# Cosine attention and a leaky-ReLU layer: a re-ordered opening, and the q and k of four batches turned on TensorE

## The chip, the cores and the metric

The kernel runs on one core of one Trainium2 chip. The metric is device time in microseconds (us). The kernel before took 509.25 us (median of 3 runs, 507.22 to 510.2).

Engines are named as in the profile: PE is TensorE (PEld its weight loads), DVE is VectorE, ACT is ScalarE, POOL is GpSimd, SP issues DMAs. In these traces each engine works through its own instructions in the order of the program (run 9 shows it for ScalarE); that is the key to most of what follows.

## The reference

```python
# q, k, v: (8 batches, 12 heads, 448 rows, 64); tau = 0.1
q_n = q / (norm(q) + 1e-6);  k_n = k / (norm(k) + 1e-6)
scores = q_n @ k_n.T / tau                      # per batch and head, 448 x 448
attn = softmax(scores);  x = attn @ v           # then heads side by side: (3584, 768)
h = x @ w_in                                    # (768, 2048)
out = maximum(0.01 * h, h) @ w_out              # (2048, 768) -> (3584, 768)
```

## The kernel before

Each batch goes through: load q, k, v (cast to bf16 by the DMA); normalise q and k (sums of squares on DVE, roots on ACT, products on POOL or DVE); turn q and k so that the 64 elements of a head lie on partitions; scores on PE; exponentials on ACT; column sums and products with V on PE; x on DVE. The two dense layers run on PE between the half-steps of the attention of a later batch. A batch has 12 half-steps, n = 0 to 11, each half of a pair of heads; four heads are a quad (three quads, g = 0 to 2).

```python
def load_w_in(a):                       # 8 transfers in all
    for s in range(2):
        nc.gpsimd.dma_start(out=w_in_sb[32*a : 32*a+32, s::2, :], in_=w_in_r[a, :, :, s, :])

def turn(b, what):                      # by DMA, a whole batch of q or k
    nc.sync.dma_start_transpose(out=xt[...], in_=xn.rearrange("p g t h d -> p (g t h d)"))

def turn_pair(b, p):                    # on PE, one pair of heads of q and k: 8 matmuls, 2 DVE copies
    tp = pmm.tile([128, 2, NT, PK], BF16, name="mm")
    ...                                 # nc.tensor.matmul(..., rhs=ident, is_transpose=True)
    nc.vector.tensor_copy(out=xt[:, g, :, j, :], in_=tp[:, i])

def weigh(b, g, s):
    if s == 0:
        sm = ppv.tile(...);  columns(sm, b, g, ones)      # 16 matmuls: the sums
        st["rs"] = wk.tile(...);  nc.vector.reciprocal(st["rs"], sm)
    po = ppv.tile(...)                                    # ppv has 2 buffers
    columns(po, b, g, v of the quad)                      # 16 matmuls: the values
    nc.vector.tensor_mul(x[:, 2*g+s, ...], po, rs)

# [... the opening: batch 0 in quads, turned by turn_pair ...]
weigh(0, 0, 0);  scores(0, 2, 1);  weigh(0, 0, 1);  scores(0, 3, 0)
# [...]
weigh(0, 2, 0);  weigh(0, 2, 1);  fill(2.0)       # three groups of the first dense layer

def second(n):                          # what batch 1 does besides: it prepares batch 2
    # [...]
    elif n == 8:
        norm_inverse(2, "q");  norm_apply(2, "q", POOL);  norm_root(2, "k")
    elif n == 9:
        norm_inverse(2, "k");  norm_apply(2, "k", DVE, step=4);  turn(2, "q")
    elif n == 10:
        turn(2, "k")

def later(b, n):                        # the same for batches 2 to 7
    if n == 0:   norm_sums(b + 1, "q")
    elif n == 1: norm_root(b + 1, "q")
    elif n == 2: load(b + 1, "v");  norm_sums(b + 1, "k");  norm_inverse(b + 1, "q");  norm_apply(b + 1, "q", POOL)
    # [... n == 3, 4: root, inverse and product of k; n == 5: turn q; n == 7: turn k ...]

# [... in every half-step n of batch b: scores; then one weigh of an earlier quad, if owed;
#      then second(n) or later(b, n); then dense groups ("fill") ...]
```

## Time and profile before

I mark progress by the start of the first exponential of each batch (in the list of ACT's instructions every 24th exponential):

| kernel before | us |
|---|---|
| batch 0 | 15.9 |
| batch 1 | 61.8 |
| batch 2 | 127.2 |
| batch 3 | 185.6 |
| batch 7 | 404.3 |
| end | 506.9 |

From batch 2 to batch 6 a batch takes 51.5 to 58.4 us. Batch 1 takes 65.4, although it has the shorter dense work. The page of the profiled execution shows where. The first line is each engine's busy time; the other two are busy tenths of TensorE, and the tenths of its clock granted, in 40 slices of 12.7 us.

```profile
PE 433.9 (86%) x3296; PEld 205.9 (41%) x3296; DVE 210.8 (42%) x218; ACT 266.0 (52%) x429; POOL 127.8 (25%) x152
...
PE   0566789850899998999799998999799999998996
...
PEclk9998699985899999999899999999999999999999
```

TensorE is near full from the twelfth slice on. It is poorly used in the first five, and the tenth shows 0: a hole from 107.9 to 126.6 us. What ended its idle times (engine and line, who released it: us in total, times, longest) names it:

```profile
PE sc L198 <- DMA kT<-k_n: 18.8, 1, 18.8
...
PE pv L209 <- DVE rs L231: 8.1, 5, 2.3
...
PE mm L253 <- DVE xT L242: 6.7, 3, 2.5
...
PE mm L172 <- POOL k_n L144: 4.3, 1, 4.3
...
PE mm L253 <- DVE xT L239: 0.9, 2, 0.4
```

The chain of waits around the hole (start, us, what):

```profile
103.21 4.97 POOL q_n L144 x3
...
108.28 3.21 SPq L161
...
113.12 13.46 DMA kT<-k_n
...
126.62 0.93 PE sc L198 x3
```

GpSimd finishes q of batch 2 at 108.2. Then SP issues the DMA that turns q, two small output stores, and at 113.12 the DMA that turns k; that one lands 13.46 us later, and only then can the scores of batch 2 begin. k itself had been normalised on DVE by 106.3; its turn waited in SP's queue.

The opening, in the timeline (start, duration, engine, line, operation, tiles, count; in brackets the idle time before it and who ended it):

```profile
25.17 0.82 POOL L90 DMA_DIRECT2D qk_bf<-in_k_dram  x1 [0.91 <-DMA w_in_sb<-in_moe_w_in_dram]
...
26.09 2.05 POOL L144 TENSOR_TENSOR k_n<-qk_bf,k_ni 112x512 bf16<-112x512 bf16 x2
...
27.21 0.55 PE L172 MATMUL mm<-ident,k_n 112*128 112x112 bf16 x4 [4.27 <-POOL k_n L144]
...
31.35 2.96 DVE L231 RECIPROCAL rs<-pv 128x448 f32<-128x448 f32 x1 [0.84 <-PE pv L209]
...
34.36 0.94 PE L209 MATMUL pv<-pe,v_bf 112*32 112x448 bf16 x16 [1.39 <-DVE rs L231]
...
35.67 3.34 ACT L202 ACTIVATE pe<-sc 112x896 bf16<-112x896 f32 x4 [1.12 <-PE sc L198]
```

GpSimd issues loads until 25.98, each behind the landing of an earlier weight transfer. Only then comes its next arithmetic, the normalisation of k of the second quad, and TensorE waits 4.27 us for it. At 31.35 the reciprocal of the first quad starts; the second values of the quad need the bank that it reads (one of the two buffers of `ppv` that TensorE writes to), so TensorE's queue stands until 34.36 and the next scores, and ScalarE behind them, with it.

### The profile page before, as it was taken

What the parts mean: (1) busy time and instruction counts of PE and PEld (TensorE: products, weight loads), DVE (VectorE), ACT (ScalarE), POOL (GpSimd) and SP (SyncE); (2) the same over time, 40 slices, a digit from 0 to 9 for tenths busy, and PEclk for the clock granted to TensorE, in tenths of its full rate; (3) what the DMA queues carried; (4) which work ended last, traced back from release to release, by engine and by line L of the source; (5) the groups of instructions that cost most, each with busy time, mean ns of one, the idle gap of its engine ahead of it and who ended that gap; (6) DMA issues with size and microseconds to landing.
All of it is one profiled execution on the core that took longest, in us unless ns stands there. A gap on an engine that the chain in (4) does not pass through costs nothing.

```text
span 506.9 us, 7801 instructions
## 1 busy us (share of the span) xinstructions
PE 433.9 (86%) x3296; PEld 205.9 (41%) x3296; DVE 210.8 (42%) x218; ACT 266.0 (52%) x429; POOL 127.8 (25%) x152
## 2 busy tenths in 40 slices
PE   0566789850899998999799998999799999998996
PEld 0232345420243453445234544444334544453463
DVE  4657577930760328332930367235633033203000
ACT  3746275530377446755566346744665557552411
POOL 7375343160046001810173004500350000000000
PEclk9998699985899999999899999999999999999999
DMA  9999948139226925293429524611442210020022
GB/s 120 212 199 203 201 57 110 31 62 199 41 43 106 135 63 87 56 163 79 71 54 120 108 51 68 104 53 49 54 78 54 60 45 1 17 60 19 1 62 64
DMA packets 79395, 42.59 MB, mean 84 GB/s; under 512 B 35072, under 2 KB 78592, under 8 KB 79360
## 3 DMA queue, kind: packets, MB, share of 16 engines
q0 software_dynamic: 37760, 22.81, 32.9%
q1 hardware_dynamic: 41600, 19.28, 17.2%
q8 instruction: 26, 0.43, 0.3%
q14 instruction: 9, 0.07, 0.0%
HBM read 45.61 MB, written 11.01 MB: 112 GB/s over the span
## 4 chain that ended last, share of the span: by engine, by line
PE 65%; DVE 13%; DMA 7%; ACT 6%; issue 4%; POOL 2%; SPq 1%; DVEq 0%; ACTq 0%; POOLq 0%
PE mm L253 25%; PE mm L265 24%; PE pv L209 10%; PE sc L198 6%; DVE rs L231 5%; ACT pe L202 3%; DMA w_in_sb<-in_moe_w_in_dram 3%; DMA kT<-k_n 3%; DVE q_ni L121 2%; DVE k_ni L121 2%; DVE q_n L112 2%; ACT hT L257 2%; POOL q_n L144 2%; DMA qk_bf<-in_q_dram 1%; DVE k_n L112 1%
## 5 line engine op out<-in xcount | busy, mean ns | idle before, releaser
L202 ACT ACTIVATE pe<-sc 112x896 bf16<-112x896 f32 x192 | 165.2, 918 | 34.0 <-PE sc L198 34.0
L253 PE MATMUL mm<-xT,w_in_sb 128*128 128x384 bf16 (+1 forms) x768 | 160.0, 359 | 13.7 <-DVE xT L242 6.7
L231 DVE RECIPROCAL rs<-pv 128x448 f32<-128x448 f32 x24 | 71.0, 2958 | 203.1 <-PE pv L209 203.1
L265 PE MATMUL mm<-w_out_sb,hT 128*128 128x384 bf16 x896 | 153.5, 327 | 0.1
L265 PEld LDWEIGHTS <-hT 128*128 128x128 bf16 x896 | 84.7, 98 | 68.5 <-issue 15.2
L253 PEld LDWEIGHTS <-w_in_sb 128*128 128x128 bf16 x768 | 72.5, 99 | 95.6 <-issue 36.6
L257 ACT ACTIVATE hT<-mm 128x384 bf16<-128x384 f32 (+1 forms) x128 | 68.9, 546 | 68.1 <-PE mm L253 67.6
L271 ACT COPY osb<-mm 128x384 f32<-128x384 f32 x56 | 26.8, 479 | 108.0 <-PE mm L265 81.2
L198 PE MATMUL sc<-qT,kT 64*128 64x448 bf16 (+1 forms) x384 | 58.6, 374 | 27.5 <-DMA kT<-k_n 18.8
L144 POOL TENSOR_TENSOR q_n<-qk_bf,q_ni 112x512 bf16<-112x512 bf16 x44 | 47.5, 1108 | 81.6 <-DVE q_ni L138 49.7
L209 PE MATMUL pv<-pe,v_bf 112*32 112x448 bf16 x768 | 48.0, 370 | 8.1 <-DVE rs L231 8.1
L90 POOL DMA_DIRECT2D v_bf<-in_v_dram x8 | 7.6, 946 | 141.8 <-PE pv L209 141.8
L144 POOL TENSOR_TENSOR k_n<-qk_bf,k_ni 112x512 bf16<-112x512 bf16 x40 | 40.5, 1043 | 11.1 <-DVE k_ni L138 8.5
L198 PEld LDWEIGHTS <-kT 64*128 64x128 bf16 (+1 forms) x384 | 14.6, 105 | 64.7 <-issue 42.7
L209 PEld LDWEIGHTS <-v_bf 112*32 112x32 bf16 x768 | 19.6, 100 | 30.4 <-issue 19.8
L121 DVE TENSOR_REDUCE q_ni<-q_n 112x16 f32<-112x1024 bf16 (+1 forms) x12 | 27.4, 2284 | 0.3
L121 DVE TENSOR_REDUCE k_ni<-k_n 112x16 f32<-112x1024 bf16 (+1 forms) x12 | 27.4, 2284 | 0.3
L209 PE MATMUL pv<-pe,ones 112*32 112x448 bf16 x384 | 25.5, 382 | 0.6 <-ACT pe L202 0.6
L242 DVE TENSOR_TENSOR xT<-pv,rs 128x448 bf16<-128x448 f32 x24 | 14.9, 621 | 8.7 <-PE pv L209 7.4
L239 DVE TENSOR_TENSOR xT<-pv,rs 128x384 bf16<-128x384 f32 x24 | 13.4, 557 | 12.3 <-PE pv L209 11.0
L172 PE MATMUL mm<-ident,q_n 112*128 112x112 bf16 x48 | 5.1, 240 | 12.8 <-DVE q_n L144 12.3
L209 PEld LDWEIGHTS <-ones 112*32 112x32 bf16 x384 | 8.4, 99 | 15.7 <-issue 12.2
(44 smaller groups left out, 129.6 us busy)
## 6 DMA issues: line engine op xcount, KB each, us to landing
v_bf<-in_v_dram POOLq DMA_DIRECT2D x8, 672.0 KB, 7.5
qk_bf<-in_q_dram POOLq DMA_DIRECT2D x6, 672.0 KB, 10.2
qk_bf<-in_k_dram POOLq DMA_DIRECT2D x6, 672.0 KB, 13.4
w_in_sb<-in_moe_w_in_dram POOLq DMA_DIRECT2D x8, 384.0 KB, 14.8
w_out_sb<-in_moe_w_out_dram POOLq DMA_DIRECT2D x2, 1536.0 KB, 22.8
out_dram<-osb SPq DMA_DIRECT2D x16, 168.0 KB, 2.2
out_dram<-osb SPq DMA_DIRECT2D x16, 144.0 KB, 2.0
out_dram<-osb SPq DMA_DIRECT2D x16, 120.0 KB, 1.9
```

The costliest lines, as they stand in the source:

```text
L112: eng.tensor_mul(sq, x, x)
L121: nc.vector.tensor_reduce(st[what + "i", b][:, 4 * g0 : 4 * g1], squares(b, what, g0, g1), axis=AX.X, op=ALU.add,)
L144: eng.tensor_tensor(out=xn[:, g, :, a : a + step, :].rearrange("p t h d -> p h t d"), in0=x[:, h : h + step], in1=ni[:, h : h + step].unsq ...
L198: nc.tensor.matmul(out=sc[:wide, a, :S], lhsT=kT[r, o : o + wide], rhs=q5[r, g, :, j, :], start=True, stop=True,)
L202: nc.scalar.activation(out=pe[:, ki], in_=sc[:PK, :, :S], func=ACTF.Exp, scale=inv_tau)
L209: nc.tensor.matmul(out=dst[32 * a : 32 * a + 32, :], lhsT=weights(a, ki), rhs=st["pe", b, 2 * g + a // 2][:, ki, a % 2, :], start=(ki == 0 ...
L231: nc.vector.reciprocal(st["rs"], sm)
L242: nc.vector.tensor_mul(x[:, kt, 64:512], po, rs)
L253: nc.tensor.matmul(out=pm[:, :n], lhsT=w_in_sb[:, kt, m * 128 : (m + 1) * 128], rhs=st["x", c][:, kt, :n], start=(kt == 0), stop=(kt == KT ...
L257: nc.scalar.activation(out=st["h", c][:, m, :n], in_=pm[:, :n], func=ACTF.Prelu, alpha=0.01)
L265: nc.tensor.matmul(out=po[:, :NH], lhsT=st["h", c][:, m, j0 : j0 + 128], rhs=w_out_sb[:, m, n * NH : (n + 1) * NH], start=(m == 0), stop=( ...
L271: nc.scalar.copy(out=osb, in_=po[:, :NH])
```

## The change

The intent: shorten the opening and remove the hole.

```diff
-    w_in_r = moe_w_in.rearrange("(g a s j) n -> a j g s n", g=G, a=4, s=2)
+    w_in_r = moe_w_in.rearrange("(a c j) n -> a j c n", a=4, c=KT)   # a quad is now heads g, 3+g, 6+g, 9+g
     def load_w_in(a):
-        for s in range(2):
-            nc.gpsimd.dma_start(
-                out=w_in_sb[32 * a : 32 * a + 32, s::2, :], in_=w_in_r[a, :, :, s, :]
-            )
+        nc.gpsimd.dma_start(out=w_in_sb[32 * a : 32 * a + 32], in_=w_in_r[a])
# [... norms, sums and products follow the new quads ...]
     norm_root(0, "q", 0, 1)
-    norm_squares(0, "q", A, 1, 2)
     norm_root(0, "k", 0, 1)
# [...]
-    weigh(0, 0, 0)
+    sm = sums(0, 0)
+    po = values(0, 0, 0)
+    inverse(0, 0, sm)
     scores(0, 2, 1)
-    weigh(0, 0, 1)
+    load_w_out(0)
+    x_write(0, 0, 0, po)
     scores(0, 3, 0)
+    x_write(0, 0, 1, values(0, 0, 1))
# [... the second quad likewise ...]
-    weigh(0, 2, 0)
-    weigh(0, 2, 1)
-    fill(2.0)
+    for m in (0, 1):
+        layer1(0, m, 0, 4)             # two dense groups, the contraction's first 4 parts of 6
+    sm = sums(0, 2)
+    po = psc.tile([128, 2, 512], F32, name="sc")
+    for s in (0, 1):
+        values(0, 2, s, po[:, s, :S])
+    inverse(0, 2, sm)
+    for s in (0, 1):
+        x_write(0, 2, s, po[:, s, :S])
+    for m in (0, 1):
+        layer1(0, m, 4, KT)            # and the last 2
# [... batch 1, n == 8 ...]
+                norm_root(2, "k")
+                norm_inverse(2, "q")
+                norm_inverse(2, "k")
+                for g in range(G):
+                    norm_apply(2, "q", P, g, g + 1)
+                    norm_apply(2, "k", V if g == 0 else P, g, g + 1)
-            turn(2, "q")
-            turn(2, "k")
# [... batch 3: sums of q at n == 3, of k at n == 5, products at n == 6 of batch 2 ...]
+    turns = {                          # (batch, half-step): (batch to turn, pairs...)
+        (1, 3): (1, 2), (1, 4): (1, 3), (1, 5): (1, 4, 5), (1, 10): (2, 0, 1),
+        (1, 11): (2, 2, 3), (2, 1): (2, 4, 5), (2, 9): (3, 0, 1), (2, 10): (3, 2, 3),
+        (2, 11): (3, 4, 5),
+    }
-        wide = 128 if b > 1 else PK
+        wide = 128 if b > 3 else PK
```

More of the change, by code (lines that the diff above doesn't have):

```diff
@@ L76, with load @@
     out_r = out.rearrange("(b p t) n -> b t p n", p=PK, t=NT)
-    w_in_r = moe_w_in.rearrange("(g a s j) n -> a j g s n", g=G, a=4, s=2)
+    w_in_r = moe_w_in.rearrange("(a c j) n -> a j c n", a=4, c=KT)
     w_out_r = moe_w_out.rearrange("(mo mi) n -> mi mo n", mi=128)
     st = {}
-    def load(b, what, h0=0, h1=H):
+    def load(b, what, g0=0, g1=G):
         src = {"q": q_r, "k": k_r, "v": v_r}[what]
@@ L89, in load @@
                 st[what, b] = bfpool.tile([PK, H, NT, D], BF16, name="qk_bf")
-        nc.gpsimd.dma_start(out=st[what, b][:, h0:h1], in_=src[b][:, h0:h1])
+        if g1 - g0 == G:
+            nc.gpsimd.dma_start(out=st[what, b], in_=src[b])
+            return
+        for g in range(g0, g1):
+            nc.gpsimd.dma_start(out=st[what, b][:, g::G], in_=src[b][:, g::G])
     def load_w_in(a):
-        for s in range(2):
-            nc.gpsimd.dma_start(
-                out=w_in_sb[32 * a : 32 * a + 32, s::2, :], in_=w_in_r[a, :, :, s, :]
-            )
+        nc.gpsimd.dma_start(out=w_in_sb[32 * a : 32 * a + 32], in_=w_in_r[a])
     def load_w_out(n):
@@ L101, in load_w_out, with by_quad, squares @@
         )
+    def by_quad(x):
+        return x.rearrange("p (a g) t d -> p g a t d", g=G)
+    def squares(b, what, g0, g1):
+        return st[what + "n", b][:, g0:g1].rearrange("p g t h d -> p g (t h d)").rearrange(
+            "p g (h t d) -> p g h t d", h=4, t=NT
+        )
     def norm_squares(b, what, eng, g0=0, g1=G):
@@ L106, in norm_squares @@
             st[what + "n", b] = inp.tile([PK, G, NT, 4, D], BF16, name=f"{what}_n")
-            st[what + "i", b] = small.tile([PK, H, NT], F32, name=f"{what}_ni")
-        x, sq = st[what, b][:, 4 * g0 : 4 * g1], squares(b, what, g0, g1)
-        if eng is nc.scalar:
-            nc.scalar.activation(sq, x, func=ACTF.Square)
-        else:
-            eng.tensor_mul(sq, x, x)
-    def squares(b, what, g0, g1):
-        return st[what + "n", b][:, g0:g1].rearrange("p g t h d -> p (g t h d)").rearrange(
-            "p (h t d) -> p h t d", h=4 * (g1 - g0), t=NT
-        )
+            st[what + "i", b] = small.tile([PK, G, 4, NT], F32, name=f"{what}_ni")
+        for g in range(g0, g1):
+            x, sq = by_quad(st[what, b])[:, g], squares(b, what, g, g + 1)[:, 0]
+            if eng is nc.scalar:
+                nc.scalar.activation(sq, x, func=ACTF.Square)
+            else:
+                eng.tensor_mul(sq, x, x)
     def norm_reduce(b, what, g0=0, g1=G):
         nc.vector.tensor_reduce(
-            st[what + "i", b][:, 4 * g0 : 4 * g1], squares(b, what, g0, g1),
+            st[what + "i", b][:, g0:g1].rearrange("p g a t -> p (g a) t"),
+            squares(b, what, g0, g1).rearrange("p g a t d -> p (g a) t d"),
             axis=AX.X, op=ALU.add,
@@ L130, in norm_root @@
     def norm_root(b, what, g0=0, g1=G):
-        ni = st[what + "i", b][:, 4 * g0 : 4 * g1]
+        ni = st[what + "i", b][:, g0:g1]
         nc.scalar.activation(ni, ni, func=ACTF.Ln, bias=tiny[:PK])
@@ L135, in norm_inverse, with norm_apply @@
     def norm_inverse(b, what, g0=0, g1=G):
-        ni = st[what + "i", b][:, 4 * g0 : 4 * g1]
+        ni = st[what + "i", b][:, g0:g1]
         nc.vector.tensor_scalar_add(ni, ni, 1e-6)
         nc.vector.reciprocal(ni, ni)
-    def norm_apply(b, what, eng, g0=0, g1=G, step=2):
-        x, xn, ni = st[what, b], st[what + "n", b], st[what + "i", b]
-        for h in range(4 * g0, 4 * g1, step):
-            g, a = divmod(h, 4)
-            eng.tensor_tensor(
-                out=xn[:, g, :, a : a + step, :].rearrange("p t h d -> p h t d"),
-                in0=x[:, h : h + step],
-                in1=ni[:, h : h + step].unsqueeze(3).to_broadcast([PK, step, NT, D]),
-                op=ALU.mult,
-            )
+    def norm_apply(b, what, eng, g0=0, g1=G):
+        x, xn, ni = by_quad(st[what, b]), st[what + "n", b], st[what + "i", b]
+        step = 4 if eng is nc.vector else 2
+        for g in range(g0, g1):
+            for a in range(0, 4, step):
+                eng.tensor_tensor(
+                    out=xn[:, g, :, a : a + step, :].rearrange("p t h d -> p h t d"),
+                    in0=x[:, g, a : a + step],
+                    in1=ni[:, g, a : a + step].unsqueeze(3).to_broadcast([PK, step, NT, D]),
+                    op=ALU.mult,
+                )
     def turned(b, what):
@@ L223, in x_place, with sums, inverse, values @@
             nc.gpsimd.tensor_copy(out=st["x", b][:, :, 0:64], in_=st["x64", b - 1])
-    def weigh(b, g, s):
-        vb = st["v", b]
-        if s == 0:
-            sm = ppv.tile([128, S], F32, name="pv")
-            columns(sm, b, g, lambda a, ki: ones[:PK, :])
-            st["rs"] = wk.tile([128, S], F32, name="rs")
-            nc.vector.reciprocal(st["rs"], sm)
-            if g == 0:
-                x_place(b)
-        rs = st["rs"]
-        po = ppv.tile([128, S], F32, name="pv")
-        columns(po, b, g, lambda a, ki: vb[:, 4 * g + a, ki, 32 * s : 32 * s + 32])
-        x, kt = st["x", b], 2 * g + s
+    def sums(b, g):
+        sm = ppv.tile([128, S], F32, name="pv")
+        columns(sm, b, g, lambda a, ki: ones[:PK, :])
+        return sm
+    def inverse(b, g, sm):
+        st["rs", b, g] = wk.tile([128, S], F32, name="rs")
+        nc.vector.reciprocal(st["rs", b, g], sm)
+        if g == 0:
+            x_place(b)
+    def values(b, g, s, po=None):
+        vb = st["v", b]
+        if po is None:
+            po = ppv.tile([128, S], F32, name="pv")
+        columns(po, b, g, lambda a, ki: vb[:, G * a + g, ki, 32 * s : 32 * s + 32])
+        return po
+    def x_write(b, g, s, po):
+        rs, x, kt = st["rs", b, g], st["x", b], 2 * g + s
         if b % 2 == 0:
@@ L242, in weigh, with layer1 @@
             nc.vector.tensor_mul(x[:, kt, 64:512], po, rs)
+    def weigh(b, g, s):
+        if s == 0:
+            inverse(b, g, sums(b, g))
+        x_write(b, g, s, values(b, g, s))
     first = [7 * (c // 2) + 3 * (c % 2) for c in range(B + 1)]
-    def layer1(c, m):
+    def layer1(c, m, k0=0, k1=KT):
         n = 128 * (first[c + 1] - first[c])
-        if m == 0:
+        if m == 0 and k0 == 0:
             st["h", c] = hpool.tile([128, MT, 512], BF16, name="hT")
-        pm = pmm.tile([128, 512], F32, name="mm")
-        for kt in range(KT):
+        if k0 == 0:
+            st["pm", m] = pmm.tile([128, 512], F32, name="mm")
+        pm = st["pm", m]
+        for kt in range(k0, k1):
             nc.tensor.matmul(
@@ L256, in layer1 @@
             )
-        nc.scalar.activation(
-            out=st["h", c][:, m, :n], in_=pm[:, :n], func=ACTF.Prelu, alpha=0.01
-        )
+        if k1 == KT:
+            nc.scalar.activation(
+                out=st["h", c][:, m, :n], in_=pm[:, :n], func=ACTF.Prelu, alpha=0.01
+            )
     def layer2(c, i, n):
@@ L305, in fill @@
             at[0] += 1
+    V, P, A = nc.vector, nc.gpsimd, nc.scalar
     make_identity(nc, ident)
     for g in range(G):
-        for what in "qk":
-            load(0, what, 4 * g, 4 * g + 4)
+        load(0, "q", g, g + 1)
+        load(0, "k", g, g + 1)
     load(0, "v")
@@ L314 @@
         load_w_in(a)
-    for what in "qk":
-        load(1, what, 0, 4)
-    for what in "qk":
-        load(1, what, 4, H)
-    V, P, A = nc.vector, nc.gpsimd, nc.scalar
+    load(1, "q", 0, 1)
+    load(1, "k", 0, 1)
     norm_squares(0, "q", V, 0, 1)
@@ L325 @@
     norm_root(0, "q", 0, 1)
-    norm_squares(0, "q", A, 1, 2)
     norm_root(0, "k", 0, 1)
-    norm_squares(0, "k", A, 1, 2)
-    norm_squares(0, "q", A, 2, 3)
-    norm_squares(0, "k", A, 2, 3)
+    for g in (1, 2):
+        norm_squares(0, "q", A, g, g + 1)
+        norm_squares(0, "k", A, g, g + 1)
     for what in "qk":
         norm_inverse(0, what, 0, 1)
-        norm_apply(0, what, V, 0, 1, 4)
+        norm_apply(0, what, V, 0, 1)
     turn_pair(0, 0)
@@ L344 @@
     norm_inverse(0, "k", 1, 2)
-    norm_apply(0, "q", V, 1, 2, 4)
+    norm_apply(0, "q", V, 1, 2)
     norm_apply(0, "k", P, 1, 2)
+    load(1, "q", 1, 3)
+    load(1, "k", 1, 3)
     norm_reduce(0, "k", 2, 3)
@@ L351 @@
     scores(0, 1, 1)
-    load_w_out(0)
-    load(1, "v")
-    load_w_out(1)
+    norm_inverse(0, "q", 2, 3)
+    norm_inverse(0, "k", 2, 3)
+    norm_apply(0, "k", P, 2, 3)
     turn_pair(0, 2)
     turn_pair(0, 3)
+    norm_apply(0, "q", V, 2, 3)
     scores(0, 2, 0)
-    norm_inverse(0, "q", 2, 3)
-    norm_inverse(0, "k", 2, 3)
-    norm_apply(0, "q", P, 2, 3)
-    norm_apply(0, "k", P, 2, 3)
-    weigh(0, 0, 0)
+    sm = sums(0, 0)
+    po = values(0, 0, 0)
+    inverse(0, 0, sm)
     scores(0, 2, 1)
-    weigh(0, 0, 1)
+    load_w_out(0)
+    x_write(0, 0, 0, po)
     scores(0, 3, 0)
+    x_write(0, 0, 1, values(0, 0, 1))
     scores(0, 3, 1)
@@ L370 @@
     norm_squares(1, "k", P, 0, 1)
+    load(1, "v")
     scores(0, 4, 0)
-    weigh(0, 1, 0)
+    sm = sums(0, 1)
+    po = values(0, 1, 0)
+    inverse(0, 1, sm)
+    x_write(0, 1, 0, po)
     scores(0, 4, 1)
-    weigh(0, 1, 1)
+    load_w_out(1)
     norm_reduce(1, "q", 0, 1)
@@ L377 @@
     scores(0, 5, 0)
+    x_write(0, 1, 1, values(0, 1, 1))
     norm_root(1, "q", 0, 1)
@@ L384 @@
     norm_apply(1, "k", P, 0, 1)
-    weigh(0, 2, 0)
-    weigh(0, 2, 1)
-    fill(2.0)
+    for m in (0, 1):
[9 more added lines that the diff above has]
+        layer1(0, m, 4, KT)
+        spent[0] += dense[m][1]
+        at[0] += 1
     turn_pair(1, 0)
     turn_pair(1, 1)
-    def second(n):
-        if n == 0:
-            load(2, "q")
-            norm_sums(1, "q", 1, 2)
-            norm_sums(1, "k", 1, 2)
-        elif n == 1:
-            load(2, "k")
-            norm_root(1, "q", 1, 2)
-            norm_root(1, "k", 1, 2)
-            norm_sums(1, "q", 2, 3)
-            norm_sums(1, "k", 2, 3)
-        elif n == 2:
-            load(2, "v")
-            for what in "qk":
-                norm_inverse(1, what, 1, 2)
-                norm_apply(1, what, P, 1, 2)
-            norm_root(1, "q", 2, 3)
-            norm_root(1, "k", 2, 3)
-        elif n == 3:
-            for what in "qk":
-                norm_inverse(1, what, 2, 3)
-                norm_apply(1, what, P, 2, 3)
-        elif n == 5:
-            load(3, "q")
-        elif n == 6:
-            norm_sums(2, "q")
-            load(3, "k")
-        elif n == 7:
-            norm_root(2, "q")
-            norm_sums(2, "k")
-        elif n == 8:
-            norm_inverse(2, "q")
-            norm_apply(2, "q", P)
-            norm_root(2, "k")
-        elif n == 9:
-            norm_inverse(2, "k")
-            norm_apply(2, "k", V, step=4)
-            turn(2, "q")
-        elif n == 10:
-            turn(2, "k")
@@ L433, in second_after, with after_scores @@
-    def second_after(n):
-        if n == 3:
-            turn_pair(1, 2)
-            turn_pair(1, 3)
-        elif n == 5:
-            turn_pair(1, 4)
-            turn_pair(1, 5)
-    def later(b, n):
-        if b + 2 < B and n < 2:
+    def after_scores(b, n):
+        if b + 2 < B and b > 1 and n < 2:
             load(b + 2, "qk"[n])
-        if b + 1 >= B:
+        if b + 1 == B:
             return
-        if n == 0:
+        if b > 1 and n == 2:
+            load(b + 1, "v")
+        if b == 1:
+            if n == 0:
+                load(2, "q")
+                norm_sums(1, "q", 1, 2)
+                norm_sums(1, "k", 1, 2)
+            elif n == 1:
+                load(2, "k")
+                norm_root(1, "q", 1, 2)
+                norm_root(1, "k", 1, 2)
+                norm_sums(1, "q", 2, 3)
+                norm_sums(1, "k", 2, 3)
+            elif n == 2:
+                load(2, "v")
+                for what in "qk":
+                    norm_inverse(1, what, 1, 2)
+                    norm_apply(1, what, P, 1, 2)
+                norm_root(1, "q", 2, 3)
+                norm_root(1, "k", 2, 3)
+            elif n == 3:
+                for what in "qk":
+                    norm_inverse(1, what, 2, 3)
+                    norm_apply(1, what, P, 2, 3)
+            elif n == 5:
+                load(3, "q")
+            elif n == 6:
+                norm_sums(2, "q")
+                load(3, "k")
+            elif n == 7:
+                norm_root(2, "q")
+                norm_sums(2, "k")
+            elif n == 8:
+                norm_root(2, "k")
[4 more added lines that the diff above has]
+                    norm_apply(2, "k", V if g == 0 else P, g, g + 1)
+        elif b == 2:
+            if n == 3:
+                norm_sums(3, "q")
+            elif n == 5:
+                norm_root(3, "q")
+                norm_sums(3, "k")
+            elif n == 6:
+                norm_root(3, "k")
+                norm_inverse(3, "q")
+                norm_inverse(3, "k")
+                for g in range(G):
+                    norm_apply(3, "q", P, g, g + 1)
+                    norm_apply(3, "k", P, g, g + 1)
+        elif n == 0:
@@ L450, in later @@
         elif n == 2:
-            load(b + 1, "v")
             norm_sums(b + 1, "k")
@@ L463, in later, with after_dense @@
             turn(b + 1, "k")
+    turns = {
[3 more added lines that the diff above has]
+    }
+    def after_dense(b, n):
+        to, *pairs = turns.get((b, n), (0,))
+        for p in pairs:
+            turn_pair(to, p)
     owed = []
@@ L476 @@
                     owed += [(b, p // 2, 0), (b, p // 2, 1)]
-                if b == 1:
-                    second(n)
-                    fill(chunk_end[0] * (n + 1) / 14)
-                    second_after(n)
-                else:
-                    later(b, n)
-                    if b == 2 and n < 2:
-                        fill(chunk_end[0] * (n + 13) / 14)
-                    else:
-                        c = b - 1 if n >= 2 else b - 2
-                        start = chunk_end[c - 1]
-                        fill(start + (chunk_end[c] - start) * ((n - 2) % 12 + 1) / 12)
+                after_scores(b, n)
+                if b == 1 or (b == 2 and n < 2):
+                    fill(chunk_end[0] * (12 * (b - 1) + n + 1) / 14)
+                else:
+                    c = b - 1 if n >= 2 else b - 2
+                    start = chunk_end[c - 1]
+                    fill(start + (chunk_end[c] - start) * ((n - 2) % 12 + 1) / 12)
+                after_dense(b, n)
     fill(spent[0] + 1.0)
```

## The prediction

> **What bounds the kernel now.** From about 145 us on, the chain of waits is almost only TensorE (dense layers, weights on V, scores), and TensorE is busy 95% or more of most stretches; nothing in the diff shortens that work. Before 145 us it is not the bound: the table of stretches gives about 95 us busy of the first 150. Two places hold the loss:
>
> 1. Opening, 0 to 61 us (first scores of batch 1 start at 61.4). ScalarE's exponentials of batch 0 need 24 x 0.87 = 20.8 us from 15.9 us on, yet end at 49.8. The timeline shows why: TensorE waits 4.3 us (22.9 to 27.2) for a turned k, because GpSimd sits in DMA issues until 25.98 (each waits for the eighth transfer before it to land); the second V product of a quad waits for the 2.97 us reciprocal to free its bank (31.4 to 34.4, 40.6 to 43.6, 50.4 to 53.4). The granted clock is 0.50 to 0.59 from 48 to 60 us.
> 2. One stall: the waits give "scores from the DMA that writes kT", 18.8 us, once. GpSimd normalises q of batch 2 until 108.2, then two DMA transposes run one after the other, the second landing at 126.6. TensorE does nothing from 107.9 to 126.6.
>
> **What the change does.** Weights in 4 transfers instead of 8 put 13, not 19, transfers before the first GpSimd normalisation: it should run at about 20 us instead of 26.1, removing the 4.3 us wait. Sums and first values of a quad come before the reciprocal, second values after the next scores: the three 1.4 to 2 us TensorE waits are hidden behind scores; in the last quad, 8 layer-1 matmuls (0.18 us each warm) run in the shadow. I work out the last exponential of batch 0 at about 44 us and the first scores of batch 1 at about 53: -8.8, less one dense item (1.06 us) that now comes later: **-7.7 us**.
>
> Turning batch 2 on TensorE by pairs, emitted after the 11th and 12th half-steps of batch 1 and the 2nd of batch 2, needs only the first quads, which the normalisation reaches about 3 us after the inverses: the wait should vanish, **-18.75 us**, all on the chain. With it goes the cold restart: after the stall 32 column matmuls take 3.4 us against 1.9 later, **-2 us**. (The Trainium skill, "TensorE: Matmul & The Clock Gate", the HAM clock gate: TensorE's clock halves after an idle window of about 3.4 us; the trace agrees, granted clock 0.50 from 126 to 130.) Norm sums of batch 3 move from half-step 0 to 3, which frees VectorE for the last x of batch 1: the 2.5 us wait at 136 to 138.5 goes, **-2.5 us**.
>
> Added: 12 turned pairs for batches 2 and 3 at about 0.6 us of TensorE, in TensorE-bound stages: **+7.4 us**; their 24 copies (0.39 us, VectorE) are off the chain, if nothing queues. Scores of batches 2 and 3 with 112 instead of 128 weight columns: 0.59 against 0.55 us per four, **+1 us**. Squares per quad instead of per batch: small, VectorE.
>
> Sum: -22.7, so about **487 us**, range 479 to 496. Chances: faster 0.93, same 0.06, slower 0.01.
>
> **What would show it.** No DMA wait on kT at batch 2; no hole near 100 us; first GpSimd normalisation near 20 us; first scores of batch 1 near 53; TensorE busy share about 89 to 90%.
>
> **What would make it wrong.** GpSimd slowed by VectorE (its 1.04 us pieces took 1.5 in the 99 to 108 us stretch) may make pairs of batch 2 wait; pairs share two banks with the dense layers; the order of landings may hold GpSimd again before the third quad; a warmer opening may gain more than I count.

## The result, and the profile after

The kernel after took 485.86 us (median of 4 runs, 484.08 to 487.51), the kernel before, with it, 509.73 (4 runs). The ratio is 0.9535, 95% interval 0.9476 to 0.9593. Here and below a ratio is that of the records, taken over the fast runs of both kernels in the same rounds, so it is not quite the ratio of the medians. Against the point forecast of about 487 the median is 1.1 us off.

The same three lines of the page:

```profile
PE 438.5 (90%) x3380; PEld 213.6 (44%) x3392; DVE 217.4 (45%) x265; ACT 265.9 (55%) x429; POOL 127.3 (26%) x152
...
PE   0786988899899989998999989997999999989996
...
PEclk9999899999999999998999999997999999998999
```

The hole is gone, TensorE's share rose from 86 to 90%, and the sum of its busy time barely moved (433.9 to 438.5). The waits of TensorE, answering to those shown before:

```profile
PE mm L274 <- ACT hT L279: 5.3, 8, 1.3
PE mm L274 <- DVE xT L253: 4.6, 5, 2.2
PE mm L274 <- DVE xT L256: 4.5, 2, 2.3
PE pv L216 <- DVE rs L239: 3.6, 2, 2.3
...
PE mm L179 <- POOL k_n L151: 0.2, 1, 0.2
```

No wait on a DMA is left in this view, and the one for GpSimd's k is down to 0.2 us. The waits for x have not become shorter in sum: 6.7 + 0.9 us before, 4.6 + 4.5 after. The longest of "xT L253", 2.2 us, is at 44.6 to 46.8 us, in the shadow of the last reciprocal of batch 0. The start of batch 2, in the timeline:

```profile
93.75 0.36 PE L179 MATMUL mm<-ident,q_n 112*128 112x112 bf16 x4
...
94.48 0.36 PE L179 MATMUL mm<-ident,q_n 112*128 112x112 bf16 x4 [0.17 <-POOL k_n L151]
...
99.30 0.59 PE L205 MATMUL sc<-qT,kT 64*112 64x448 bf16 x4
```

The first two pairs of batch 2 are turned 5 us before their scores; the second of them waited 0.17 us for GpSimd. And the opening:

```profile
18.80 2.82 POOL L151 TENSOR_TENSOR k_n<-qk_bf,k_ni 112x512 bf16<-112x512 bf16 x2 [6.11 <-DVE k_ni L144]
...
22.26 0.58 PE L179 MATMUL mm<-ident,k_n 112*128 112x112 bf16 x4
...
25.05 2.05 POOL L151 TENSOR_TENSOR k_n<-qk_bf,k_ni 112x512 bf16<-112x512 bf16 x2
...
25.84 2.96 DVE L239 RECIPROCAL rs<-pv 128x448 f32<-128x448 f32 x1 [0.99 <-PE pv L216]
...
27.87 5.13 ACT L209 ACTIVATE pe<-sc 112x896 bf16<-112x896 f32 x6 [2.31 <-PE sc L205]
...
29.97 0.94 PE L216 MATMUL pv<-pe,v_bf 112*32 112x448 bf16 x16
```

GpSimd's first normalisation starts at 18.80 instead of 26.09. The Trainium skill, "GPSIMD Engine Reference", section "1. Specifications", says that GpSimd shares its SBUF interfaces with VectorE, and that VectorE instructions with two SBUF inputs contend for them. The trace agrees: the two pieces took 2.82 us at 18.80, beside VectorE's product of q (18.56 to 19.72), and 2.05 us at 25.05. The reciprocal of 25.84 to 28.80 has scores and exponentials beside it, and the second values at 29.97 wait for nothing. ScalarE still stands 2.31 us here.

| first exponential of | before | after | difference |
|---|---|---|---|
| batch 0 | 15.9 | 14.7 | -1.2 |
| batch 1 | 61.8 | 50.6 | -11.2 |
| batch 2 | 127.2 | 99.7 | -27.5 |
| batch 3 | 185.6 | 159.7 | -25.9 |
| batch 6 | 346.8 | 321.9 | -24.9 |
| batch 7 | 404.3 | 381.5 | -22.8 |
| end | 506.9 | 485.3 | -21.6 |

So 27.5 us are won by the start of batch 2 and about 6 given back later, in these two executions.

### The profile page after: what moved, and what is told of

It reads as the page before. It is cut to its first block, busy times and chain, and to the rows that moved or that the text cites. A ratio compares the mean times of both kernels' runs of the same rounds, so it can differ in the third digit from the quotient of the medians.

```text
span 485.3 us, 8021 instructions
## 1 busy us (share of the span) xinstructions
PE 438.5 (90%) x3380; PEld 213.6 (44%) x3392; DVE 217.4 (45%) x265; ACT 265.9 (55%) x429; POOL 127.3 (26%) x152
## 4 chain that ended last, share of the span: by engine, by line
PE 70%; DVE 14%; ACT 8%; issue 5%; POOL 1%; DMA 1%; DVEq 0%; ACTq 0%; POOLq 0%
PE mm L274 26%; PE mm L287 25%; PE pv L216 10%; PE sc L205 7%; DVE rs L239 5%; ACT pe L209 4%; DVE q_n L123 2%; DVE q_ni L126 2%; ACT hT L279 2%; DVE k_ni L126 2%; PE mm L179 2%; POOL q_n L151 1%; DVE k_n L123 1%; DMA qk_bf<-in_q_dram 1%; ACT osb L293 1%
## 5 line engine op out<-in xcount | busy, mean ns | idle before, releaser
L274 PE MATMUL mm<-xT,w_in_sb 128*128 128x384 bf16 (+1 forms) x756 | 161.9, 362 | 16.2 <-ACT hT L279 5.3
L209 ACT ACTIVATE pe<-sc 112x896 bf16<-112x896 f32 x192 | 165.0, 917 | 15.0 <-PE sc L205 14.9
L287 PEld LDWEIGHTS <-hT 128*128 128x128 bf16 x896 | 84.6, 98 | 67.8 <-issue 14.5
L151 POOL TENSOR_TENSOR q_n<-qk_bf,q_ni 112x512 bf16<-112x512 bf16 x42 | 43.5, 1063 | 92.1 <-DVE q_ni L144 37.0
L205 PE MATMUL sc<-qT,kT 64*112 64x448 bf16 (+1 forms) x384 | 59.6, 379 | 8.8 <-ACT pe L209 5.4
L151 POOL TENSOR_TENSOR k_n<-qk_bf,k_ni 112x512 bf16<-112x512 bf16 x44 | 45.4, 1059 | 16.8 <-DVE k_ni L144 12.4
L216 PE MATMUL pv<-pe,v_bf 112*32 112x448 bf16 x736 | 44.1, 360 | 3.6 <-DVE rs L239 3.6
L91 POOL DMA_DIRECT2D v_bf<-in_v_dram x8 | 7.6, 949 | 110.5 <-PE pv L216 82.9
L205 PEld LDWEIGHTS <-kT 64*112 64x112 bf16 (+1 forms) x384 | 16.4, 113 | 42.6 <-issue 38.0
L216 PEld LDWEIGHTS <-v_bf 112*32 112x32 bf16 x768 | 18.9, 97 | 23.8 <-issue 12.3
L216 PE MATMUL pv<-pe,ones 112*32 112x448 bf16 x384 | 23.6, 364 | 0.0
L179 PE MATMUL mm<-ident,q_n 112*128 112x112 bf16 x96 | 9.9, 233 | 12.7 <-DVE q_n L151 11.1
L189 DVE COPY qT<-mm 128x448 bf16<-128x448 bf16 x24 | 9.3, 387 | 25.6 <-PE mm L179 25.3
L256 DVE TENSOR_TENSOR xT<-pv,rs 128x448 bf16<-128x448 f32 x24 | 15.0, 623 | 9.9 <-PE pv L216 8.3
L253 DVE TENSOR_TENSOR xT<-pv,rs 128x384 bf16<-128x384 f32 x22 | 12.2, 556 | 12.7 <-PE pv L216 11.6
## 6 DMA issues: line engine op xcount, KB each, us to landing
w_out_sb<-in_moe_w_out_dram POOLq DMA_DIRECT2D x2, 1536.0 KB, 19.3
```

The source lines that it names most:

```text
L151: eng.tensor_tensor(out=xn[:, g, :, a : a + step, :].rearrange("p t h d -> p h t d"), in0=x[:, g, a : a + step], in1=ni[:, g, a : a + step ...
L179: nc.tensor.matmul(out=tp[:, i, t, :], lhsT=xn[:, g, t, 2 * j : 2 * j + 2, :].rearrange("p h d -> p (h d)"), rhs=ident, is_transpose=True, ...
L205: nc.tensor.matmul(out=sc[:wide, a, :S], lhsT=kT[r, o : o + wide], rhs=q5[r, g, :, j, :], start=True, stop=True,)
L209: nc.scalar.activation(out=pe[:, ki], in_=sc[:PK, :, :S], func=ACTF.Exp, scale=inv_tau)
L216: nc.tensor.matmul(out=dst[32 * a : 32 * a + 32, :], lhsT=weights(a, ki), rhs=st["pe", b, 2 * g + a // 2][:, ki, a % 2, :], start=(ki == 0 ...
L256: nc.vector.tensor_mul(x[:, kt, 64:512], po, rs)
```

## The experiments

My theory had two parts that add: the hole at batch 2 is the DMA turn (about 19 us), and the opening was held by GpSimd's place behind transfers and by the reciprocal's bank (about 8 us). The rivals: the hole is really the late normalisation; or the hole's end is set by the DMA queues, so that a quicker opening only makes it longer. Times are medians; "kernel before" beside them is that of the same rounds.

### 1. The turn of batch 2 alone

The kernel before, with this:

```diff
         elif n == 8:
+            norm_root(2, "k"); norm_inverse(2, "q"); norm_inverse(2, "k")
+            # products by quads: q on POOL; k of quad 0 on DVE, of quads 1 and 2 on POOL
-        elif n == 9:  # ... turn(2, "q")
-        elif n == 10: # ... turn(2, "k")
+        # pairs 0, 1 after n == 10, pairs 2, 3 after n == 11, pairs 4, 5 after n == 1 of batch 2
+        # batch 2 prepares batch 3 two half-steps later (the tile is read by pairs 4, 5 until then)
+        wide = 128 if b > 2 else PK
```

> The kernel before with one part of the change: batch 2 turned by pairs on TensorE (and, as that needs it, the normalisation of batch 3 two half-steps later). Theory (the DMA turn of batch 2 is the stall): the 18.8 us wait for kT goes, the cold restart (2 us) and the 2.5 us wait for x go, six pairs cost 6 x 0.65 = 3.9 us: about -19 us, 490 us; first exponentials of batch 2 at about 110 us instead of 127.2. Rival (the stall is really the late normalisation on GpSimd, finished at 108.2): TensorE waits for the pairs instead, at least 8 us of the stall stay, 498 us or more.

Measured: 492.28 us against 509.55; ratio 0.9645 (0.9582 to 0.9708), that is -18.1 us of 509.55. First exponentials of batch 2 at 108.8. The DMA wait is gone, and no more than 0.1 us of waiting for POOL's q or k of batch 2 took its place. The theory holds against this rival: GpSimd ended its part at 108.57 us here and at 108.17 in the kernel before, and yet the hole is gone. So the hole was the wait for the DMA turn of the whole batch. Turning in pairs does two things at once, as it also lets the scores start when one quad is ready; a DMA turn by quads was not tried.

### 2. The opening alone

The kernel after, with batches 2 and 3 prepared and turned by DMA as before, and `wide = 128 if b > 1`.

> The kernel after, with batches 2 and 3 turned by DMA as before: the new opening alone. Theory (the two gains add): first exponentials of batch 1 at 50.6 us, the stall of about 18.8 us stays, first exponentials of batch 2 at about 117; time about 509.7 - 10.2 = 499.5 us. Rival (the transposes end at a time set by the DMA queues, so a quicker opening is eaten by a longer stall): first exponentials of batch 2 still at 125 or later, time over 506 us.

Measured: 502.34 us against 509.55; ratio 0.9867 (0.9777 to 0.9957), -6.8 us; its four runs spread from 498.33 to 505.42. In the profile the first exponentials of batch 1 are at 50.5, TensorE's wait on kT is 19.4 us, and the first exponentials of batch 2 are at 117.2. (The profiled execution is the fastest of the four. By their times alone the records call this run unclear; it is the profile that decides.) The rival falls: the hole moved with the opening. The two parts add: 18.1 + 6.8 = 24.9 us against 23.7 us for both (1 - 0.9535 of 509.73), within the intervals, which are wide.

### 3. Does the load of batch 4 stretch the turn?

The kernel before, with one line:

```diff
-        if b + 2 < B and n < 2:
-            load(b + 2, "qk"[n])
+        if b + 2 < B and (n in (2, 3) if b == 2 else n < 2):
+            load(b + 2, "qk"[n % 2])
```

> The kernel before, with the loads of q and k of batch 4 issued two half-steps later, behind the transposes of batch 2. In the kernel before the q transpose took 4.9 us and the k transpose 13.5, while these loads ran. Theory A (the loads share the DMA engines with the k transpose and stretch it): the k transpose takes 6 to 8 us, the stall falls from 18.8 to about 12, time about 503 us. Theory B (a transpose takes that long by itself): stall 18 to 19 us, time as before within 1 us.

(The 4.9 us for q in this text is the distance between the two issues. From issue to landing q took 10.2 us in the kernel before, 108.2 to 118.4.)

Measured: 505.69 us against 509.55; ratio 0.9914 (0.985 to 0.9978). Neither number came: the result lies between the theories. In the chain of waits the k transpose takes

```profile
113.85 10.24 DMA kT<-k_n
```

instead of 13.46 us, and the wait on kT is 15.4 us instead of 18.8. But the edit did only half of what it was meant to do. In its trace GpSimd, with nothing else in its queue, issued the load of q at 109.33, right behind the q transpose; only the load of k moved, to 147.72. So the fifth of the hole that went belongs to one of the two loads. How long the hole would be with neither was not run, but the kernel before shows it of other batches. Its last four transposes (from 317.4 us), with no load under way, landed 5.0 to 6.8 us after their issue, and the q transposes of batches 3 to 5 after 5.0; the k transposes of batches 3 to 5, each with the loads of q and k issued beside it (from 158.74 on for the first), took 9.6 to 10.4. So Theory A deserves more weight than the run gave it: two transposes of 5 us, one behind the other, would have been an estimated 10 us.

The Trainium skill, "DMA: Bandwidth & Descriptors", section "Latency and other measured facts", gives 261 GB/s for a transposing DMA with a non-contiguous middle dimension, and about 350 to 400 for a contiguous one. One q or k here is 112 x 3072 elements of 2 bytes, 688 KB, which at the lower rate would be an estimated 2.6 us. No transpose came near it: 5.0 us is 137 GB/s, and 13.46 us is 51 GB/s. The measurement decides.

### 4. Is turning batch 3 on TensorE worth it?

The kernel after, with `turn(3, "q")` at n == 7 and `turn(3, "k")` at n == 8 of batch 2 instead of the six pairs, and `wide = 128 if b > 2`.

> The kernel after, with batch 3 alone turned by DMA again (q after half-step 7, k after 8 of batch 2), in a stage where TensorE is the bound. Theory (turning batch 3 on TensorE costs its work and saves nothing): six pairs at 0.65 us and the 112-column scores go, -4 us, about 482 us, no wait on kT. Rival (the transposes land late or collide with the loads of batch 4): a wait on kT at the start of batch 3, time 486 us or more.

Measured: 484.64 us against 509.55; ratio 0.9502 (0.9441 to 0.9564). That is not separable from the kernel after (0.9535). In the profile the k transpose took 14.48 us this time, and TensorE waited:

```profile
PE sc L205 <- DMA kT<-k_n: 3.8, 1, 3.8
```

So the rival's wait came, and it ate the 3.7 us that the pairs cost (six pairs at 0.62 us; in the kernel after two pairs hold TensorE 1.21 to 1.33 us from their first matmul to the next scores). A draw. Batch 3 has to be normalised late because its tile is read by the last pairs of batch 2, and that leaves the DMA too little time; both loads of batch 4 ran beside it as well (issued at 141.26 and 142.23).

### 5. Eight weight transfers again

```diff
-        nc.gpsimd.dma_start(out=w_in_sb[32 * a : 32 * a + 32], in_=w_in_r[a])
+        for s in range(2):
+            nc.gpsimd.dma_start(
+                out=w_in_sb[32 * a : 32 * a + 32, 3 * s : 3 * s + 3],
+                in_=w_in_r[a, :, 3 * s : 3 * s + 3])
```

> The kernel after with the first weights in 8 transfers again. Theory (GpSimd's place behind transfers that wait for landings was the 4.3 us wait): the normalisation of k of the second quad starts about 22 us instead of 18.8 and TensorE waits 2 to 3 us for its turned pair; first exponentials of batch 1 at 52 to 54 instead of 50.6; time 487.5 to 490 us. Rival (the other moves of the opening hide it): 50.6 within 0.7, time as after, 485 to 487.

Measured: 487.91 us (487.74 to 489.31) against 508.66; ratio 0.9596 (0.9575 to 0.9617). The timeline shows the mechanism:

```profile
22.87 2.05 POOL L155 TENSOR_TENSOR k_n<-qk_bf,k_ni 112x512 bf16<-112x512 bf16 x2
...
23.98 0.56 PE L183 MATMUL mm<-ident,k_n 112*128 112x112 bf16 x4 [2.19 <-POOL k_n L155]
...
26.13 1.72 ACT L213 ACTIVATE pe<-sc 112x896 bf16<-112x896 f32 x2 [3.00 <-PE sc L209]
```

GpSimd's normalisation slipped from 18.80 to 22.87, TensorE waited 2.19 us for it, ScalarE 3.00. The half-step that took 2.5 us in the kernel after (21.3 to 23.8) took 4.7 (21.4 to 26.1), and the first exponentials of batch 1 came at 52.7. That part of the theory is shown. It is worth about 2.2 us, not the 4.3 that I read as one wait in the kernel before. The rest of the way from 26.09 to 22.87 is the two loads of batch 1 that the change moved behind this normalisation, and the earlier start; neither has a run of its own.

### 6. The old order of sums, values and reciprocal

The kernel after, with `weigh(0, g, 0)` and `weigh(0, g, 1)` back at their old places for the first two quads.

> The kernel after with the first two quads of batch 0 weighed in the order of before: sums, reciprocal, both value products at fixed places, the second behind the bank that the reciprocal frees. Theory: the wait for the reciprocal (about 1.5 to 2 us a quad) comes back on TensorE and ScalarE's exponentials slip: first exponentials of batch 1 3 to 4 us later, at about 54; time about 489 us. Rival (ScalarE has slack): 50.6 within 0.7.

Measured: 488.63 us (487.01 to 488.8) against 508.66; ratio 0.9594 (0.9568 to 0.962). First exponentials of batch 1 at 54.6, 4.0 us later than after. Around the second reciprocal:

```profile
36.11 1.69 PE L216 MATMUL pv<-pe,ones 112*32 112x448 bf16 x16
...
37.85 2.96 DVE L239 RECIPROCAL rs<-pv 128x448 f32<-128x448 f32 x1 [1.97 <-PE pv L216]
...
39.79 1.72 ACT L209 ACTIVATE pe<-sc 112x896 bf16<-112x896 f32 x2 [2.22 <-PE sc L205]
...
40.86 0.94 PE L216 MATMUL pv<-pe,v_bf 112*32 112x448 bf16 x16 [0.93 <-DVE rs L239]
```

The values at 40.86 waited until the reciprocal ended, and each exponential group here starts 3.9 and 2.4 us after the one before it, where the kernel after has 2.1 and 1.6. The theory holds, but not all of the 4.0 us is the order. The first line shows the sums of this quad at 1.69 us; in the kernel after they took 0.94 (at 33.46). TensorE's matmuls became quick at about 39.5 us in this execution and at about 27.6 in the kernel after. Runs 8 and 10, with the new order and a similar slow stretch, lost some 2.3 us by it, so an estimated 2 us are left for the order; the medians say 2.0 (against the yardstick of run 11) to 2.8. Whether the old order itself keeps the matmuls slow for longer is not shown.

### 7. The last quad and the dense groups unsplit

The kernel after, with `weigh(0, 2, 0)`, `weigh(0, 2, 1)`, `fill(2.0)` in place of the split groups.

> The kernel after with the last quad and the first dense groups in the order of before: sums, values, values, then three dense groups whole. Theory: the 8 matmuls at 0.18 us and the second value product no longer run in the shadow of the reciprocal; one more dense group (1.06 us) runs before batch 1: first exponentials of batch 1 3.5 us later (54), of which 1.06 is only moved: time about +2.4, 488 us. Rival (the split buys nothing but moves work): first exponentials 1.1 us later, time as after.

Measured: 489.63 us (486.88 to 490.92) against 508.66; ratio 0.9617 (0.9578 to 0.9656). First exponentials of batch 1 at 54.2; but those of batch 0 were 1.0 us late in this execution, which the edit can't cause.

```profile
43.39 2.96 DVE L239 RECIPROCAL rs<-pv 128x448 f32<-128x448 f32 x1 [1.38 <-PE pv L216]
...
46.40 1.68 PE L216 MATMUL pv<-pe,v_bf 112*32 112x448 bf16 x16 [2.29 <-DVE rs L239]
...
48.02 4.58 PE L274 MATMUL mm<-xT,w_in_sb 128*128 128x384 bf16 x18
```

TensorE waits 2.29 us in the reciprocal's shadow. The kernel after waits there too, 2.20 us ("xT L253" at 46.78), but has the second values behind it already, and its 8 dense matmuls ran before the sums (39.24 and 40.97), while exponentials were awaited. From the last half-step of batch 0 (41.2) to batch 1 it took 13.0 us against 9.7; about 1.1 us of that is the third dense group, which is only moved. So some 2.2 us are real, as expected. The clock does not explain them: 6.8 us at half clock fall into this stretch here and 3.4 in the kernel after, but the yardstick of run 11 has 6.8 too and takes 9.7.

### 8. One root moved

```diff
     norm_root(0, "q", 0, 1)
+    norm_squares(0, "q", A, 1, 2)
     norm_root(0, "k", 0, 1)
```

> The kernel after with one ScalarE instruction pair moved: the root of k of the first quad behind the squares of q of the second quad, which wait for their load. Theory (in the kernel before this order held the first scores back): first exponentials of batch 0 at 15.6 to 15.9 instead of 14.7, those of batch 1 about 1.2 us later, time +1.2. Rival (the 1.2 us between the two profiles are the landings of that execution): 14.7 to 15.1, no change.

Measured: 487.72 us (485.18 to 489.81) against 508.66; ratio 0.9584 (0.9544 to 0.9625).

```profile
10.07 1.06 ACT L121 ACTIVATE q_n<-qk_bf 112x1024 bf16<-112x1024 bf16 x1 [1.96 <-DMA qk_bf<-in_q_dram]
...
11.03 0.29 ACT L138 ACTIVATE k_ni<-k_ni,tiny 112x16 f32<-112x16 f32 x1
```

The square waits for its load until 10.07 and the root of k stands behind it until 11.03; in the kernel after the root ran at 9.42. The first exponentials came at 15.4, 0.7 us after those of the kernel after. But other executions with the new order started between 14.7 and 15.7. So the order costs some of the 1.2 us; the rest of that difference is how the first loads landed. Batch 1 began 3.0 us late in this run, more than the edit explains: three half-steps between 30 and 38 us were slower, and TensorE's matmuls in them too (the sums of the second quad took 1.23 us, 0.94 in the kernel after). Run 10, whose opening is that of the kernel after, shows the same slow stretch (1.2 us; batch 1 at 53.1), so it comes with the execution. The records of the clock show nothing in this stretch, but the matmuls do: four scores take 1.00 us until 35.1 and 0.59 at 38.0 in this run, and the switch comes between 36 and 37 us, against about 27.6 in the kernel after. I take this to be TensorE's clock rising later. The Trainium skill, "TensorE: Matmul & The Clock Gate", section "What's actually happening", says that the window over which the clock is decided is free-running, which would give such differences.

Runs 5 to 8 all have medians 2 to 4 us above the kernel after. Their intervals overlap those of the kernel after (0.9476 to 0.9593, and 0.954 to 0.9622 when repeated), so for each of them it is the timeline, not the total, that carries the verdict.

### 9. The same idea in batches 4 and 6

In the prediction I had credited the change with a 2.5 us wait of TensorE for the last x of batch 1, held in DVE's queue behind the norm sums of batch 3. The kernel after still has two such waits ("xT L256", 2 times, 4.5 us) in batches 4 and 6, where the old schedule remains. So I moved those too:

```diff
-        elif n == 0:
+        elif n == (1 if b % 2 == 0 else 0):
             norm_sums(b + 1, "q")
         elif n == 1:
             norm_root(b + 1, "q")
         elif n == 2:
+            if b % 2 == 0:
+                norm_root(b + 1, "q")
             norm_sums(b + 1, "k")
```

> The kernel after with one more move: in batches 4 and 6 the norm sums of the next q (5.1 us of VectorE) come one half-step later, behind the last x of the batch before. Theory (the two waits of TensorE for that x, 2.3 us each, are VectorE's order, as the one that the change removed in batch 2): both go, -4.6 us, about 481 us. Rival (the wait only moves, to the next reciprocal or to the DMA turn of q): time as after, 485 to 486.

Measured: 487.03 us (486.33 to 488.56) against 509.44; ratio 0.9567 (0.9541 to 0.9593). Nothing gained. The wait for x went; this came:

```profile
220.47 3.35 DVE L126 TENSOR_REDUCE q_ni<-q_n 112x48 f32<-112x3072 bf16 x1
...
223.92 0.34 ACT L138 ACTIVATE q_ni<-q_ni,tiny 112x48 f32<-112x48 f32 x1 [3.52 <-DVE q_ni L126]
...
225.07 2.72 PE L274 MATMUL mm<-xT,w_in_sb 128*128 128x512 bf16 x6 [3.16 <-ACT hT L279]
```

ScalarE now stands 3.52 us at the root of q, whose sums end at 223.8. The dense layer's eviction (the activation that empties its bank) stands behind that root in ScalarE's queue, so TensorE gets no bank and waits 3.16 us. The Trainium skill, "TensorE: Matmul & The Clock Gate", section "Architectural detail", calls ScalarE and VectorE strict FIFO; this trace agrees.

### 10. Both: late sums, and batch 3 by DMA

As run 9, with the six pairs of batch 3 replaced by DMA turns at n == 5 and 7, and the last pairs of batch 2 one half-step earlier.

> As the run before it, and batch 3 turned by DMA with its normalisation two half-steps earlier than in the kernel after (the last two pairs of batch 2 are turned one half-step earlier to free the tile). Theory (a DMA turn costs TensorE nothing if it has landed in time): the 3.8 us wait on kT of the run with batch 3 by DMA goes, the 3.9 us of pairs stay away: about 477 us. Rival (the pairs of batch 2 now wait for GpSimd, or the k transpose still lands late): 481 us or more.

Measured: 488.05 us (487.66 to 491.91) against 509.44; ratio 0.9597 (0.9569 to 0.9626). A miss: it carries the flaw of run 9 in three batches (waits for "ACT hT" 14.9 us, 5.3 in the kernel after). No wait on kT is left in its list, but what batch 3 by DMA is worth stays open, because the new wait covers it.

### 11 and 12. The roots moved as well

The kernel after, unchanged, as a yardstick in the same rounds:

> The kernel after, unchanged, in the same rounds as the next run: a yardstick. Expected: ratio to before 0.950 to 0.957, 484 to 488 us; first exponentials of batch 1 between 49.5 and 53.5 us (other executions of this same opening gave 49.6 to 53.1).

Measured: 486.67 us (484.85 to 489.42) against 509.15; ratio 0.9581 (0.954 to 0.9622); first exponentials of batch 1 at 50.3.

And the kernel after with each root a half-step or more behind its sums in batches 4 and 6:

```diff
+        elif b % 2 == 0 and n < 5:
+            if n == 1:
+                norm_sums(b + 1, "q")
+            elif n == 2:
+                norm_sums(b + 1, "k")
+            elif n == 3:
+                norm_root(b + 1, "q");  norm_inverse(b + 1, "q");  norm_apply(b + 1, "q", P)
+            elif n == 4:
+                norm_root(b + 1, "k");  norm_inverse(b + 1, "k");  norm_apply(b + 1, "k", P)
```

> The kernel after, in batches 4 and 6 with the sums of q one half-step later and the two roots each a half-step later again, so that neither VectorE holds the last x of the batch before nor ScalarE stands at a root whose sums are not done. Theory (in the run with late sums the wait moved to ScalarE's root, in order before the dense layer's evictions; both waits are order, and each also costs a 3.4 us window at half clock behind it): both 2.3 us waits go and the half-clock windows near 222 and 332 us with them: -4.6 to -8 us against the yardstick, 478 to 482 us. Rival (one of the three engines always ends up holding the chain there): within 1.5 us of the yardstick.

Measured: 477.93 us (475.69 to 481.42) against 509.15; ratio 0.9405 (0.9361 to 0.9448), below the yardstick's interval; the medians differ by 8.7 us. Of TensorE's waits for x and for evictions this is left, and "xT L256" is gone:

```profile
PE mm L274 <- DVE xT L253: 4.8, 5, 2.2
PE mm L274 <- ACT hT L279: 4.1, 6, 1.3
```

Batches 4 and 6 each take 54.4 us, first exponential to first exponential, against 58.5 and 59.6 in the kernel after: 4.1 and 5.2 us each, for a wait of 2.3. A part of the surplus is the clock, and run 5 tells how much: it has the old order in these batches and no half clock in them, and takes 57.6 us for each. So 3.2 us are mostly waits (in run 5, 2.27 for x and 0.60 for the eviction behind it), and the remaining 0.9 and 2.0 us go with the half clock. Stretches of the kernel after around those waits (busy us of PE, PEld, DVE, ACT, POOL with counts; granted clock; DMA share; GB/s):

```profile
218.90:222.30 3.40, 1.08 (x5) 0.42 (x5) 3.40 (x3) 0.63 (x3) 0.00 (x0) 1.00 0.95 115
222.30:225.70 3.40, 3.40 (x9) 1.18 (x8) 3.37 (x4) 2.55 (x4) 0.00 (x0) 0.50 0.65 87
328.10:331.50 3.40, 1.50 (x6) 0.60 (x7) 3.37 (x2) 0.35 (x1) 0.98 (x1) 1.00 0.56 71
```

After a 3.4 us stretch in which TensorE was busy 1.08 us, the next 3.4 us ran at 0.50 of the clock; the same followed the stretch at 328.1, for 6.8 us. In this kernel's profile no half-clock stretch lies between 55 and 280 us. This version beats both kernels.

## Why the prediction was right

- **The hole.** Predicted -18.75 us with the wait gone. The wait is gone, and run 1, which does little else, gave -18.1 us net (interval 14.9 to 21.3). For its parts I had added up -19.3: the hole -18.75, the restart -2, the wait for x -2.5, six pairs +3.9. The mechanism is shown.
- **The cold restart.** Predicted -2. The half clock from 110.5 to 131.0 us of the kernel before has no counterpart in the kernel after; that the restart alone was 2 us was not measured by itself.
- **The opening.** Predicted -7.7, first scores of batch 1 at about 53. They came at 49.97 (first exponentials -11.2, less 1.06 for the dense group that comes later: -10.1). This term was under-sized by about 2.4 us in the profiles. A likely reason is one that the prediction names among its risks, a warmer opening: the half clock around the end of batch 0 lasted 13.7 us in the kernel before (45.6 to 59.3) and 3.4 in the kernel after (48.2 to 51.6). The 18 matmuls of the first dense groups took 5.16 us before, an estimated 3.2 at the 0.18 us each of full clock. No run separates this. Its parts as measured: transfers about 2.2 (run 5), order of sums, values and reciprocal an estimated 2 (run 6), split about 2.2 (run 7; not by dense matmuls in the reciprocal's shadow, as predicted: the wait there stays 2.20 us), the root up to 0.7 (run 8, a part that I had missed in the diff). The timed run of the opening alone gave -6.8 with an interval of -11.4 to -2.2, which holds both figures.
- **The wait for x.** Predicted -2.5. It went in batch 2, but ScalarE's root at about 129 us made a wait of 1.3 us ("ACT hT") in its place. Run 9 shows that such an exchange can eat the whole gain, and run 12 that it need not.
- **The pairs.** Predicted +7.4 for twelve at 0.6 us. Two pairs hold TensorE 1.21 to 1.33 us in the trace, 7.5 us for twelve: right. That batch 3 pays for itself is not shown: run 4 is a draw.
- **The 112-column scores.** Predicted +1; not measured by itself.
- **What was not foreseen.** The kernel after loses about 4 us from batch 3 to the end against the kernel before, in these profiles. Its stretches at half clock there sum to 13.6 us, those of before to 3.4 (the last 2.5 us of both aside). Ten more microseconds at half the clock are an estimated 5 us of matmuls at most, so this is a likely cause. At the price seen in run 12 (0.9 us for a stretch of 3.4, 2.0 for one of 6.8) it would be an estimated 3 of the 4 us; the rest is open. It falls differently in each execution: the yardstick has 10.2 us.

The mechanism of the larger term, the hole, was right. That the sum was right to 1.1 us is luck: the opening gave more than I counted, and the later stages took some of it back.

## What to carry to other kernels

A transfer by DMA that must land before the next stage can start is paid in full when its source is ready late, and more when loads run beside it (5.0 us became 9.6 to 14.5 here); turning on TensorE in small pieces costs its 0.6 us a piece and lets the stage start with the first piece. When a wait is removed by moving one engine's instruction, look for the engine that waits for that instruction in order: the sums that left DVE's queue stood in ScalarE's as a root. A short wait of TensorE in a dense stage can cost more through the half clock behind it: 0.9 and 2.0 us here, beside 3.2 us of waiting for each of two batches. Removing both was worth 8.7 us between the medians.

## What the Trainium skill lacked or had wrong

- "TensorE: Matmul & The Clock Gate" says that the clock falls after an idle window of about 3.4 us and advises against idle gaps longer than about 3 us. Here gaps of 2.3 us sufficed in the kernel after: the half clock followed stretches of 3.4 us in which TensorE had been busy 1.08 us (218.9), 1.50 us (328.1) and 1.09 us (433.9). They did not always: none followed the gaps of 2.27 us at 222.7 and 332.9 in run 5, nor one of 3.00 us at 125.6 in run 2. The page tells of another kernel whose short idles throttled it, but doesn't say how busy a window has to be. Its length agrees: the half-clock stretches last 3.4, 6.8, 10.2, 13.7, 17.1 or 20.5 us in the runs.
- "DMA: Bandwidth & Descriptors" gives 261 GB/s for a transposing DMA with a non-contiguous middle dimension, and about 350 to 400 otherwise. 688 KB took 5.0 to 14.5 us from issue to landing here, 137 to 47 GB/s. How much ordinary loads stretch a transpose is on no page: in the kernel before k took 5.0 us with no load beside it (377.53), 9.6 with the loads of q and k issued beside it (158.74), and 13.46 with these loads, two stores and the q transpose under way (113.12).
